# Channel 128's rows by one 89-column matmul a batch, read back once behind the last transform; E and O columns in two tiles

## The chip, the cores and the metric

The kernel runs on one core of a Trainium2 chip. The metric is the device time of one execution in microseconds (us), the median of several runs. The profile is one execution on that core. Its engines are PE (matmuls), PEld (loads of the weight block that a matmul holds still, beside PE), DVE (vector), ACT (scalar), POOL, and SP, which here only issues transfers. "Start-to-start" below is the time from the start of one matmul to the start of the next, read from the start times in the trace. Every run was a fast one, with a mean granted matmul clock of 0.992 or more.

## The reference

```python
def _attn_ref(x):                       # x: 8 x 3008 x 256
    X = np.fft.fft(x, axis=1)
    X = np.fft.fft(X, axis=2)
    return X.real.astype(np.float32)

def _moe_ref(x, w_gate, w_val, w_out):  # x: 24064 x 256, hidden size 1536
    g = x @ w_gate
    gelu = 0.5 * g * (1.0 + erf(g * inv_sqrt2))
    val = x @ w_val
    return (gelu * val @ w_out).astype(np.float32)
```

A two-dimensional Fourier transform per batch, its real part, and a gated feed-forward block on every token.

## The kernel before

The kernel keeps half of the transformed sequence, as even (E) and odd (O) channel parts. From one pair of products it gets a token and its mirror image. Channel 128 belongs to the even side, but it is stored in row 0 of O. Its row is also spread over all 128 partitions (EB), and DVE uses it with one weight per partition (yw) to mend the mirrored value.

The work of the feed-forward block is cut into 288 blocks, 36 a batch (three groups of columns by twelve slices of the hidden size). A block is five matmuls of 512 or 481 columns (L660) and eight of 256 (L749). The transform of the next batch is strewn between them: in each block, behind its matmuls, stand the "fill" steps planned for it. POOL first "folds" the input (sums and differences); `s1t` is the first half of the transform; its result goes through memory and comes back as Z; `tp_e` and `tp_o` make the second half from Z, one each for each of three groups. Where a batch's number stands below beside a stretch of blocks, it is the batch whose transform stands there: batch 4 is blocks 108 to 144. For batches 1 to 7 channel 128 went like this:

```python
    def tp_y(b, gi):                    # once for each of three groups
        ...
            nc.tensor.matmul(
                ps[:4, 0:128], _sub(st["Z"], [[C, 4]], 4 * gi * C + 128), _sub(TP, [[1, 128]], 0),
                start=True, stop=True)
            yr = yrow_tile()
            nc.scalar.activation(yr[:, :], ps[:4, 0:128], AF.Copy)
            y = yrow_dram[b % 2]
            nc.sync.dma_start(
                out=ap_replace(y, ap=[[128, 4], [1, 128]], offset=y.offset + chunk_off[gi]), in_=yr[:, :])

    def tp_rows(b, gi):                 # a block behind the group's tp_o
        ...
            nc.sync.dma_start(out=_sub(EB_bufs[b], [[1, n]], chunk_off[gi]), in_=ap_replace(y, ap=[[0, 128], [1, n]], offset=o))
            nc.sync.dma_start(out=_sub(EO_bufs[b], [[1, n]], HALF + chunk_off[gi], part_num=1), in_=...)
```

The weight block of that matmul is four columns of Z: channel 128 of each of a group's four pairs of sequence positions, 256 elements apart. So a batch has three such matmuls, three evictions by ACT, three row writes to memory and six reads.

## Time and profile before

| | before |
|---|---|
| median of the runs | 630.14 us (629.61 to 630.75) |
| span in the profile | 627.0 us |
| PE, DVE, POOL, ACT busy | 98%, 92%, 81%, 68% |
| a block without fill (512, 481 columns) | 1.95 us, 1.90 us |
| 36 blocks, with the transform of batch 4, 5 or 6 | 73.9 us |
| row matmuls | 21, by shape 128*4 x 128 columns |

The first three lines show a kernel that is bound by its matmul stream. The block times are differences of the starts of each block's first gelu in the trace.

### The profile page before, as it was taken

What the parts mean: (1) busy time and instruction counts of PE and PEld (TensorE: products, weight loads), DVE (VectorE), ACT (ScalarE), POOL (GpSimd) and SP (SyncE); (2) the same over time, 40 slices, a digit from 0 to 9 for tenths busy, and PEclk for the clock granted to TensorE, in tenths of its full rate; (3) what the DMA queues carried; (4) which work ended last, traced back from release to release, by engine and by line L of the source; (5) the groups of instructions that cost most, each with busy time, mean ns of one, the idle gap of its engine ahead of it and who ended that gap; (6) DMA issues with size and microseconds to landing.
All of it is one profiled execution on the core that took longest, in us unless ns stands there. A gap on an engine that the chain in (4) does not pass through costs nothing.

```text
span 627.0 us, 12895 instructions
## 1 busy us (share of the span) xinstructions
PE 612.3 (98%) x4195; PEld 405.1 (65%) x4243; DVE 578.3 (92%) x941; ACT 428.4 (68%) x842; POOL 505.3 (81%) x510
## 2 busy tenths in 40 slices
PE   7999999999999999999999999999999999999997
PEld 3456666666666666666666666666666666666666
DVE  8689989999899999999999998999999999999992
ACT  6777677666776677667676677676676666666661
POOL 8399999989897998879997899969988655555651
PEclk8999999999999999999999999999999999999999
DMA  9961754536353353731645335633212322221123
GB/s 177 227 97 31 210 129 116 144 105 159 99 146 101 98 133 79 184 113 46 160 110 135 101 78 127 148 97 98 62 49 63 91 86 55 51 52 39 42 51 81
DMA packets 54217, 65.40 MB, mean 104 GB/s; under 512 B 7831, under 2 KB 49802, under 8 KB 51754
## 3 DMA queue, kind: packets, MB, share of 16 engines
q1 hardware_dynamic: 47222, 49.03, 30.6%
q0 software_dynamic: 6608, 15.29, 11.4%
q8 instruction: 33, 0.54, 0.4%
q10 hardware_dynamic: 320, 0.26, 0.2%
q14 instruction: 34, 0.28, 0.2%
HBM read 39.65 MB, written 30.17 MB: 111 GB/s over the span
## 4 chain that ended last, share of the span: by engine, by line
PE 93%; ACT 2%; issue 1%; DVE 1%; DMA 1%; POOL 1%; POOLq 0%; ACTq 0%
PE ps_o L749 38%; PE ps_g L660 28%; PE ps_v L660 19%; PE ps_dft L546 2%; PE ps_dft L582 2%; PE ps_o L820 1%; DMA Z_sb<-z 1%; PE ps_dft L443 1%; PE ps_dft L612 0%; ACT gelu_sb L676 0%; POOL h_sb L724 0%; POOL eo_sb L224 0%; DMA out_dram<-out_sb 0%; ACT gelu_sb L685 0%; PE ps_dft L749 0%
## 5 line engine op out<-in xcount | busy, mean ns | idle before, releaser
L724 POOL TENSOR_TENSOR h_sb<-gelu_sb,v_sb 128x512 bf16<-128x512 bf16 (+1 forms) x280 | 319.8, 1146 | 93.1 <-DVE v_sb L722 85.9
L749 PE MATMUL ps_o<-Wo_sb,h_sb 128*128 128x256 bf16 (+1 forms) x2232 | 334.9, 273 | 0.9 <-POOL h_sb L724 0.9
L749 PEld LDWEIGHTS <-h_sb 128*128 128x128 bf16 (+1 forms) x2304 | 228.7, 100 | 112.9 <-POOL h_sb L724 2.6
L676 ACT ACTIVATE gelu_sb<-ps_g 128x512 bf16<-128x512 f32 (+1 forms) x288 | 169.4, 588 | 98.6 <-PE ps_g L660 80.9
L660 PE MATMUL ps_g<-EO_sb,W_sb 128*128 128x512 bf16 (+1 forms) x817 | 228.5, 375 | 3.8 <-ACT gelu_sb L685 0.8
L704 DVE SCALAR_TENSOR_TENSOR ve_sb<-EB_sb,yw,ps_v 128x512 f32<-128x512 bf16 (+1 forms) x280 | 206.3, 737 | 25.9 <-PE ps_v L660 25.0
L660 PE MATMUL ps_v<-EO_sb,W_sb 128*128 128x512 bf16 (+1 forms) x575 | 213.7, 375 | 0.7 <-DVE W_sb L451 0.6
L720 DVE TENSOR_TENSOR h_sb<-gelu_sb,ps_v 128x512 bf16<-128x512 bf16 (+1 forms) x280 | 189.9, 678 | 1.1 <-ACT gelu_sb L685 0.7
L660 PEld LDWEIGHTS <-W_sb 128*128 128x128 bf16 x1440 | 137.2, 98 | 81.1 <-issue 1.8
L722 DVE SCALAR_TENSOR_TENSOR v_sb<-ve_sb,ps_v 128x512 f32<-128x512 f32 (+1 forms) x280 | 187.5, 670 | 0.0
L685 ACT ACTIVATE gelu_sb<-ps_g 128x512 bf16<-128x512 f32 (+1 forms) x288 | 168.7, 586 | 0.0
L769 ACT ACTIVATE out_sb<-ps_o 128x512 f32<-128x512 f32 x92 | 55.0, 598 | 35.7 <-PE ps_o L749 35.6
L224 POOL TENSOR_TENSOR eo_sb<-ab_sb 94x512 bf16<-94x512 f32 (+1 forms) x70 | 77.6, 1111 | 0.5
L549 ACT ACTIVATE S_sb<-ps_dft 96x512 bf16<-96x512 f32 x56 | 32.9, 588 | 14.0 <-PE ps_dft L546 13.9
L592 ACT ACTIVATE EO_sb<-ps_dft 128x512 bf16<-128x512 f32 (+1 forms) x44 | 26.0, 590 | 23.3 <-PE ps_dft L582 22.1
L217 POOL TENSOR_TENSOR ab_sb<-x_raw,x_raw 94x508 f32<-94x508 f32 (+1 forms) x30 | 33.0, 1100 | 0.0
L220 POOL TENSOR_TENSOR ab_sb<-x_raw,x_raw 94x508 f32<-94x508 f32 (+1 forms) x30 | 32.9, 1098 | 0.0
L546 PE MATMUL ps_dft<-eo_sb,G 94*96 94x256 bf16 x119 | 22.5, 274 | 0.2 <-POOL eo_sb L224 0.2
L158 POOL DMA_INDIRECT x_raw<-in_x_dram,idx x18 | 17.1, 948 | 2.9 <-issue 1.1
L582 PE MATMUL ps_dft<-TP,Z_sb 128*128 128x128 bf16 (+1 forms) x184 | 17.8, 218 | 0.0
L582 PEld LDWEIGHTS <-Z_sb 128*128 128x128 bf16 x192 | 14.6, 98 | 1.8 <-DVE Z_sb L534 0.6
L546 PEld LDWEIGHTS <-G 94*96 94x96 bf16 x119 | 13.0, 123 | 1.2 <-issue 0.4
(148 smaller groups left out, 166.2 us busy)
## 6 DMA issues: line engine op xcount, KB each, us to landing
out_dram<-out_sb SPq DMA_DIRECT2D x364, 64.0 KB
x_raw<-in_x_dram SPq DMA_DIRECT2D x10, 768.0 KB
Z_sb<-z SPq DMA_DIRECT2D x7, 768.0 KB
z<-S_sb SPq DMA_DIRECT2D x7, 576.0 KB
EB_sb<-yrow SPq DMA_DIRECT2D x14, 128.0 KB
z<-S_sb SPq DMA_DIRECT2D x7, 192.0 KB
x_raw<-in_x_dram SPq DMA_DIRECT2D x2, 640.0 KB
EB_sb<-yrow SPq DMA_DIRECT2D x7, 120.2 KB
```

The lines of the kernel that those rows point to most:

```text
L224: eng.tensor_tensor(_sub(eo, [[C, nj], [1, 128]], j0 * C + g * 128), ab(0, 0, [[1, 128]]), ab(1, 0, [[1, 128]]), op=op)
L546: nc.tensor.matmul(ps[:96, q * C : (q + 1) * C], G[:, j, :], _sub(eo, [[1, C]], j * C), start=(j == js[0]), stop=(j == js[-1]))
L582: nc.tensor.matmul(ps[:, o : o + n], st["Z"][:, pair, g * 128 : g * 128 + 128], _sub(TP, [[1, n]], g * 128), start=True, stop=True)
L660: nc.tensor.matmul(ps[:, :n], W[nm, part][:, fs], src, start=start, stop=stop, **kw)
L676: nc.scalar.activation(gl[:, 0, :n], pg[:, :n], AF.Gelu)
L685: nc.scalar.activation(_sub(gl, [[-1, n]], TOK + n - 1), pg[:, :n], AF.Gelu)
L704: nc.vector.scalar_tensor_tensor(ve[:, :n], EB_bufs[b][:, c0 : c0 + n], yw[:, fc : fc + 1], pv[:, :n], op0=ALU.mult, op1=ALU.add)
L720: nc.vector.tensor_tensor(st["h"][:, fc, 0, :n], gl[:, 0, :n], pv[:, :n], op=ALU.mult)
L722: nc.vector.scalar_tensor_tensor(_sub(vv, [[-1, n]], n - 1), ve[:, :n], 2.0, pv[:, :n], op0=ALU.mult, op1=ALU.subtract)
L724: nc.gpsimd.tensor_tensor(st["h"][:, fc, 1, :n], gl[:, 1, :n], vv[:, :n], op=ALU.mult)
L749: nc.tensor.matmul(pso[:m, half], st["h"][:, fc, sign, h0 : h0 + m], Wo_sb[:, fc, :], start=(fc == 0 and not (first and sign)), stop=(fc = ...
L769: nc.scalar.activation(_sub(osb, [[1, 2 * C]], 0, part_num=m), pso[:m, :], AF.Copy)
```

## The change

The intent: fewer, wider matmuls for channel 128, fewer transfers, and no wait between transforms and the row's read. There are four parts, of which the fourth is a rearrangement of the plan.

```diff
-    def EO_tile():
-        return work([128, 2, HALF], BF16, "EO", 2, "EO_sb")
+    def EO_tiles():
+        return [work([128, HALF], BF16, t, 2, t + "_sb") for t in ("E", "O")]
...
+    YS = C // 32
+    YM = YS * (NK // 2 - 1) + 1
...
+    def tp_row(b):
+            ps = psum("dft")
             nc.tensor.matmul(
-                ps[:4, 0:128], _sub(st["Z"], [[C, 4]], 4 * gi * C + 128), _sub(TP, [[1, 128]], 0),
+                ps[:YM, 0:128], _sub(st["Z"], [[C // YS, YM]], 128), _sub(TP, [[1, 128]], 0), start=True, stop=True)
             yr = yrow_tile()
-            nc.scalar.activation(yr[:, :], ps[:4, 0:128], AF.Copy)
+            nc.scalar.activation(yr[:, :], ps[:YM, 0:128], AF.Copy)
...
-    def tp_rows(b, gi):
+    def tp_rows(b, c0, n):
...
-    def make_yw(f0, n):                 # four groups, in blocks 0, 1, 2 and 5
+    def make_yw():                      # all twelve, in block 6
...
-            items = []
-            for gi in range(NG):
-                items += [tp_y(b, gi), tp_e(b, gi), tp_o(b, gi)]
+            items = [tp_row(b)] + [f(b, gi) for gi in range(NG) for f in (tp_e, tp_o)]
...
+            if b > 1:
+                at(fill, s + 1, tp_rows(b, 0, HALF))
...
-            first, n = {2: (s0 - 13, 29), 3: (s0 - 19, 30)}.get(b, (s0 - 22, 32))
+            first, n = {2: (s0 - 10, 27), 3: (s0 - 19, 30)}.get(b, (s0 - 22, 32))
...
                 for g in range(2):
                     s = max(s + 1, ready)
+                    while s in taken:
+                        s += 1
                     at(fill, s, s1t(b, jg, g))
```

The wanted rows are 12, one for each pair. The matmul takes 89 columns of Z, 32 elements apart, so every eighth row of its result is wanted and 77 are thrown away. For batch 1 the rows are still read in three pieces. In the opening, two evictions move from DVE to ACT and some output pieces move by a block.

More of the change, by code (lines that the diff above doesn't have):

```diff
@@ L123, in EB_tile @@
         return work([128, HALF], BF16, "EB", 2, "EB_sb")
+    YS = C // 32
+    YM = YS * (NK // 2 - 1) + 1
     def yrow_tile():
-        return work([4, 128], BF16, "yrow", 2, "yrow_sb")
+        return work([YM, 128], BF16, "yrow", 2, "yrow_sb")
     def gelu_tile():
@@ L247 @@
     NGP = NJ * NK
-    ff = work([128, 2 * NGP], FP32, "EO", 2, "ff")
-    rr = work([128, 2 * NGP], FP32, "EO", 2, "rr")
+    ff = work([128, 2 * NGP], FP32, "E", 2, "ff")
+    rr = work([128, 2 * NGP], FP32, "O", 2, "rr")
     rd = work([128, 2 * NGP + NK], FP32, "Z", 1, "rd")
@@ L466, in make_w @@
         return run
-    def make_yw(f0, n):
+    def make_yw():
         def run():
-            c0, nq = f0 // 128, n // 128
             ps = psum("dft")
-            for i in range(nq):
+            for i in range(NFC):
                 nc.tensor.matmul(
-                    ps[:, i : i + 1], W["v", "O"][0:1, f0 + i * 128 : f0 + (i + 1) * 128], one_h,
-                    start=True, stop=True)
-            nc.scalar.activation(yw[:, c0 : c0 + nq], ps[:, 0:nq], AF.Copy)
+                    ps[:, i : i + 1], W["v", "O"][0:1, i * 128 : (i + 1) * 128], one_h, start=True, stop=True)
+            nc.scalar.activation(yw[:, :], ps[:, 0:NFC], AF.Copy)
         return run
@@ L578, in run @@
             if b not in EO_bufs:
-                EO_bufs[b] = EO_tile()
+                EO_bufs[b] = EO_tiles()
             ps = psum(tag) if tag else ps_any(b)
@@ L589, in run @@
             n = chunk_len[gi]
-            dst = _sub(EO_bufs[b], [[1, n]], g * HALF + chunk_off[gi])
+            dst = _sub(EO_bufs[b][g], [[1, n]], chunk_off[gi])
             if engine == "A":
@@ L602, in run @@
             n = chunk_len[gi]
-            eb = _sub(EB_bufs[b], [[1, n]], chunk_off[gi])
             ps = ps_any(b)
-            if b == 0:
-                for pair, o, w in pairs(gi):
-                    nc.tensor.matmul(
-                        ps[:, o : o + w], _sub(st["Z"], [[0, 128]], pair * C + 128), _sub(TP, [[1, w]], 0),
-                        start=True, stop=True)
-                nc.scalar.activation(eb, ps[:, :n], AF.Copy)
-                return
+            for pair, o, w in pairs(gi):
+                nc.tensor.matmul(
+                    ps[:, o : o + w], _sub(st["Z"], [[0, 128]], pair * C + 128), _sub(TP, [[1, w]], 0),
+                    start=True, stop=True)
@@ L612, in run @@
+            nc.scalar.activation(_sub(EB_bufs[b], [[1, n]], chunk_off[gi]), ps[:, :n], AF.Copy)
+        return run
+    def tp_row(b):
+        def run():
+            st = state(b)
+            EB_bufs[b] = EB_tile()
+            ps = psum("dft")
             nc.tensor.matmul(
-                ps[:4, 0:128], _sub(st["Z"], [[C, 4]], 4 * gi * C + 128), _sub(TP, [[1, 128]], 0),
-                start=True, stop=True)
+                ps[:YM, 0:128], _sub(st["Z"], [[C // YS, YM]], 128), _sub(TP, [[1, 128]], 0), start=True, stop=True)
@@ L615, in run @@
             yr = yrow_tile()
-            nc.scalar.activation(yr[:, :], ps[:4, 0:128], AF.Copy)
+            nc.scalar.activation(yr[:, :], ps[:YM, 0:128], AF.Copy)
             y = yrow_dram[b % 2]
+            step = yr.ap[0][0]
             nc.sync.dma_start(
-                out=ap_replace(y, ap=[[128, 4], [1, 128]], offset=y.offset + chunk_off[gi]), in_=yr[:, :])
+                out=ap_replace(y, ap=[[128, NK // 2], [1, 128]], offset=y.offset),
+                in_=ap_replace(yr, ap=[[YS * step, NK // 2], [1, 128]]))
@@ L620, in tp_y @@
         return run
-    def tp_rows(b, gi):
+    def tp_rows(b, c0, n):
         def run():
-            n, y = chunk_len[gi], yrow_dram[b % 2]
-            o = y.offset + chunk_off[gi]
-            nc.sync.dma_start(
-                out=_sub(EB_bufs[b], [[1, n]], chunk_off[gi]), in_=ap_replace(y, ap=[[0, 128], [1, n]], offset=o))
-            nc.sync.dma_start(
-                out=_sub(EO_bufs[b], [[1, n]], HALF + chunk_off[gi], part_num=1),
-                in_=ap_replace(y, ap=[[0, 1], [1, n]], offset=o))
+            y = yrow_dram[b % 2]
+            for dst, rows in ((EB_bufs[b], 128), (EO_bufs[b][1], 1)):
+                nc.sync.dma_start(
+                    out=_sub(dst, [[1, n]], c0, part_num=rows),
+                    in_=ap_replace(y, ap=[[0, rows], [1, n]], offset=y.offset + c0))
@@ L663, in cols_of @@
             n, c0 = chunk_len[ci], chunk_off[ci]
-            E, O = (EO_bufs[b][:, i, c0 : c0 + n] for i in range(2))
+            E, O = (EO_bufs[b][i][:, c0 : c0 + n] for i in range(2))
             if ci not in cstate:
@@ L872, in behind_first_gate @@
     def behind_first_gate():
-        make_yw(0, 256)()
         tp_y(0, 0)()
@@ L886, in plan @@
         for gi in (1, 2):
-            early += [ch(0, 2 * gi), ch(0, 2 * gi + 1, "V"), tp_e(0, gi), tp_o(0, gi, "V"), tp_y(0, gi)]
+            e = "A" if gi == 1 else "V"
+            early += [ch(0, 2 * gi), ch(0, 2 * gi + 1, e), tp_e(0, gi), tp_o(0, gi, e), tp_y(0, gi)]
         for s, f in (
-                (0, make_w(0, 256, 256)), (0, make_w(1, 256, 256, engine="V")), (1, make_yw(256, 256)),
-                (1, make_w(1, 512, 512, (1,))), (2, make_w(0, 512, 512, (0,), "V")), (2, make_yw(512, 512)),
+                (0, make_w(0, 256, 256)), (0, make_w(1, 256, 256, engine="V")),
+                (1, make_w(1, 512, 512, (1,))), (2, make_w(0, 512, 512, (0,), "V")),
                 (3, make_w(0, 512, 512, (1,))), (3, make_w(1, 512, 512, (0,), "V")),
-                (4, make_w(1, 1024, 512, (1,), "V")), (5, make_w(0, 1024, 512, (0,), "V")), (5, make_yw(1024, 512)),
-                (6, make_w(0, 1024, 512, (1,))), (7, make_w(1, 1024, 512, (0,), "V"))):
+                (4, make_w(1, 1024, 512, (1,), "V")), (5, make_w(0, 1024, 512, (0,), "V")),
+                (6, make_w(0, 1024, 512, (1,))), (6, make_yw()), (7, make_w(1, 1024, 512, (0,), "V"))):
             at(fill, s, f)
@@ L901, in plan, with spread @@
             at(fill, s, lambda k=k: load_part(2, k, (load_mirror,)))
-        def spread(b, items, s0, s1):
-            each = len(items) // NG
+        taken = set()
+        def spread(b, s0, s1):
+            items = [tp_row(b)] + [f(b, gi) for gi in range(NG) for f in (tp_e, tp_o)]
             for i, f in enumerate(items):
-                s = s0 + i * (s1 - s0) // (len(items) - 1)
+                s = s0 + (i * (s1 - s0) // (len(items) - 1) if b > 1 else (0, 2, 3, 6, 8, 11, 13)[i])
                 at(fill, s, f)
-                if i % each == each - 1:
-                    at(fill, s + 1, tp_rows(b, i // each))
+                taken.add(s)
+                if b == 1 and i and i % 2 == 0:
+                    at(fill, s + 1, tp_rows(b, chunk_off[i // 2 - 1], chunk_len[i // 2 - 1]))
+            if b > 1:
+                at(fill, s + 1, tp_rows(b, 0, HALF))
         for b in range(1, B):
@@ L937, in plan @@
             at(fill, s + 2, z_read(b))
-            items = []
-            for gi in range(NG):
-                items += [tp_y(b, gi), tp_e(b, gi), tp_o(b, gi)]
             if b == 1:
-                spread(b, items, s + 6, s + 18)
+                spread(b, s + 7, s + 20)
                 continue
             assert s + 7 < s0 + NS - 10
-            spread(b, items, s + 7, s0 + NS - 3)
+            spread(b, s + 7, s0 + NS - 5 if b == 2 else s0 + NS - 6)
         return fill, pool
@@ L957, in feed @@
         first = works[0]
-        sooner = {8: [first[0]], 9: [first[3]], 10: [first[1]], 11: [first[4]], 13: [first[2]], 14: [first[5]]}
+        sooner = {9: [first[0]], 10: [first[3]], 11: [first[1]], 12: [first[4]], 13: [first[2]], 14: [first[5]]}
         works[0] = first[6:]
```

## The prediction

> **What bounds the kernel now.** I read the page first, by engine, then the chain of waits that ended last, then the timeline of a quiet stretch at 290 us, then the list of waits.
>
> ```profile
> PE 612.3 (98%) x4195; PEld 405.1 (65%) x4243; DVE 578.3 (92%) x941; ACT 428.4 (68%) x842; POOL 505.3 (81%) x510
> ...
> PE 93%; ACT 2%; issue 1%; DVE 1%; DMA 1%; POOL 1%; POOLq 0%; ACTq 0%
> PE ps_o L749 38%; PE ps_g L660 28%; PE ps_v L660 19%; PE ps_dft L546 2%; PE ps_dft L582 2%; PE ps_o L820 1%; DMA Z_sb<-z 1%; PE ps_dft L443 1%; PE ps_dft L612 0%; ACT gelu_sb L676 0%; POOL h_sb L724 0%; POOL eo_sb L224 0%; DMA out_dram<-out_sb 0%; ACT gelu_sb L685 0%; PE ps_dft L749 0%
> ```
>
> The matmul engine is busy 98% of 627.0 us and makes 93% of the chain. So the time is the length of the matmul stream: what leaves that stream leaves the time, and what leaves ACT, DVE or the DMA queue counts only where the stream was waiting for it. The row matmuls of channel 128 (L612) look like nothing, 0% of the chain. Their true cost is in the start times of their neighbours:
>
> ```profile
> 291.23 0.60 PE L749 MATMUL ps_o<-Wo_sb,h_sb 128*128 128x256 bf16 x4
> ...
> 291.67 0.39 PE L582 MATMUL ps_dft<-TP,Z_sb 128*128 128x128 bf16 x4
> ...
> 291.89 0.81 PE L660 MATMUL ps_g<-EO_sb,W_sb 128*128 128x512 bf16 x3
> ...
> 293.41 0.60 PE L749 MATMUL ps_o<-Wo_sb,h_sb 128*128 128x256 bf16 x4
> ...
> 293.85 0.81 PE L660 MATMUL ps_g<-EO_sb,W_sb 128*128 128x512 bf16 x3
> ...
> 295.37 0.60 PE L749 MATMUL ps_o<-Wo_sb,h_sb 128*128 128x256 bf16 x4
> ...
> 295.90 0.09 PEld L612 LDWEIGHTS <-Z_sb 128*4 128x4 bf16 x1 [0.21 <-issue]
> 295.90 0.22 PE L612 MATMUL ps_dft<-TP,Z_sb 128*4 128x128 bf16 x1
> ...
> 296.05 0.52 PEld L660 LDWEIGHTS <-W_sb 128*128 128x128 bf16 x4
> 296.05 0.80 PE L660 MATMUL ps_g<-EO_sb,W_sb 128*128 128x481 bf16 x3
> ```
>
> Columns are start and duration in us. Four L749 matmuls with nothing behind them take 293.85 - 293.41 = 0.44 us up to the next L660. With four full transforms (L582) between, 0.66: the four cost 0.22, or 56 ns each. With one row matmul of 4 weight columns between, 0.68: that one costs 0.24. Its weight load stands at 295.90 beside its own matmul, with 0.21 us of idle weight loading before it, where the L749 and L582 loads were done ahead. Over all 21 row matmuls the median start-to-start is 203 ns from the last L749 to L612 (L749 to L582: 109) and 154 ns from L612 to L660 (L582 to L660: 56). So each adds 203 + 154 - 109 = 248 ns, some 190 ns of it for being narrow.
>
> The by-shape groups show that 96 columns are not narrow in this sense, and the list of waits adds up the idle loads and shows one false wait:
>
> ```profile
> L546 PE MATMUL ps_dft<-eo_sb,G 94*96 94x256 bf16 x119 | 22.5, 274 | 0.2 <-POOL eo_sb L224 0.2
> ...
> PEld L612 <- issue: 4.2, 20, 0.2
> ...
> ACT EO_sb L592 <- DMA EO_sb<-yrow: 1.1, 2, 0.6
> ```
>
> L546 (96 weight columns) follows L749 at 109 ns and is followed by L660 at 108 ns, just its own 256 streamed columns: no extra. Idle before the 4-column loads is 0.2 us in 20 cases of 21. In the third line ACT waits to write E or O columns for a row still being read into row 0 of the shared tile.
>
> **What the Trainium skill says.** "TensorE: Matmul & The Clock Gate", section "Back-to-back issue gap", gives N/2.4 + 2.5 ns warm. The trace agrees: 56 ns at 128 columns, 109 at 256, 216 at 512. "TensorEngine Tiling (Array Packing)", section "Key Properties", says: "Mode switching requires drain"; its "Available Configurations" have column tiles of 32, 64 and 128. Four columns would take the 32-column form, 89 the full one. The trace agrees with a drain on the way in (203 for 109) and out (154 for 56), for the 1-column weights of L587 too (136 in, 151 out), and none for 96. The first page's section "Weight-path perf modes" reserves the fast weight load for 128 weights; the trace has 98 ns for 128 columns and 123 ns for the 96 of L546, so 89 columns should load in about 0.12 us (estimate). A stride of 32 elements between weight columns is in no load here.
>
> **The change part by part.**
>
> 1. *Row matmuls.* 3 per batch become 1, for 7 batches; the instruction order of the changed program shows 14 matmuls and 14 weight loads fewer. Removed: 21 x 248 ns = 5.2 us. Added: 7 matmuls of 128 streamed columns, 56 ns each, if no drain comes with 89 columns. Since the matmul is shorter than a weight load, I add some 25 ns for the load of its successor: 7 x 80 ns = 0.6 us. All on the bounding engine: **-4.6 us**.
> 2. *make_yw.* Four groups of 1-row matmuls become one of 12. Entering such a group costs 312 ns where a 512-column matmul alone gives 216 (+96); leaving it takes 91 where the inner ones take 26 (+65). Three groups fewer: 3 x 0.16 = **-0.5 us**, at 19 to 33 us, where the stream waits little.
> 3. *ACT evictions.* 14 of 0.25 us (row) and 3 of yw go; two DVE copies of 0.68 us move to ACT. ACT is busy 68%; only single waits count. **About 0**.
> 4. *E and O in two tiles.* At 160.76 ACT had waited 0.61 us for the row of O before writing E; ACT's two gelus slid, and the stream stood from 162.08 to 162.81, where 0.11 would do. The row now comes after the last transform and E has its own tile: **-0.6 us**, once.
> 5. *Batch 1's slots.* Its first transform step comes one block later. At 80.04 the stream waited 0.26 us for Z's read; that goes. The folds of batch 2 start three blocks later (26 for 23): at 76.94 an L749 waited 1.06 us for POOL, behind those folds. I count half: together **-0.8 us**.
> 6. *DMA.* 14 row writes and 24 row reads fewer; the transfers lie beside compute: **0**, unless the late read is late (below).
> 7. *Opening.* yw leaves ACT, `sooner` and the evictions are shuffled; one ACT wait of 0.33 us at 25.5 may go, others may appear: **0.4 us longer** together with any new wait at a batch's start, as a guard.
>
> Sum: -4.6 - 0.5 - 0.6 - 0.8 + 0.4 = -6.1 us. From 630.1: **624.0 us**, 1.0% less.
>
> **The rivals.**
>
> *The late read becomes a wait.* Rows of batch 2 are read in block 68 and needed in block 72; those of batches 3 to 7 in blocks 103, 139 and so on, needed five blocks later. A block is 1.95 us or more, so there are at least 6 us, then 8. Now, a third of the row (128 KB) has its last packet started 1.3 to 2.7 us after issue, and Z's 768 KB landed 4.2 us after issue, so 376 KB should need 3 us (estimate). Issue usually comes within 1 us of the block's end, but was 3.4 and 4.9 us late in blocks 95 and 100, once behind a row write caught by an input load (5.1 us). That would just touch the deadline in batch 3. If the read is late by 2 us in each of six batches, 12 us come back: about 630. I give this 8%.
>
> *89 strided columns load slowly or drain.* If each new row matmul still costs 250 ns, 1.2 us come back; if a strided load takes 0.4 us, 2 us. Then about 625.5. Against it: L546.
>
> *DVE becomes the bound.* It is busy 92%. Its three operations of a block sum to 2.09 us (737 + 678 + 670 ns), over the 1.95 of a block without extras, yet they overlap by some 0.09 us each: starts at 289.55, 290.15, 290.78. In the last batch, where no transform stands between, the stream still runs at 1.95 us a block, against this rival. It would matter only if blocks fell below 1.9. The gain comes from blocks of 2.2 us and over, so it holds: 5% for losing 2 us.
>
> *Much more comes back.* For a gain over 2% the time must fall below 617.5. All waits of the stream outside the opening that I can name are under 4 us, and part 1 is limited to 5.2. Very unlikely.
>
> **Range and chances.** Part 1 lies between -4.0 and -5.0, the waits between +1 and -3. So 621.8 to 627.0 holds eight times in ten; the spread of the runs before (629.6 to 630.8) adds little. Within 2%: 96%; faster by over 2%: 3%; slower: 1%.
>
> **What the new profile would show.** Part 1: seven row matmuls with 128*89 weights, 109 ns behind L749 and 55 to 110 ns before L660, no idle "issue" line for their loads. Part 2: one yw group. Part 4: no wait of ACT for the row of O, and no 0.7 us stop near 162. Part 5: no stop at 77 and 80. From batch 4 on, a batch, now 73.9 us from start to start, should take 73.3: less 3 x 0.248, plus 0.08. I would be wrong if the O matmul that opens a batch waits for the row's read, if the new row matmul keeps a gap of 0.2 us, or if the opening gets longer by a microsecond or more.

## The result, and the profile after

| | before | after |
|---|---|---|
| median of four runs each | 630.14 us | 623.78 us (622.64 to 624.27) |
| span in the profile | 627.0 us | 620.6 us |

The ratio of the times is 0.9896, 95% interval 0.9879 to 0.9913. Ratios here are the mean time of one kernel's fast runs over that of the other's fast runs of the same rounds, so not quite the ratio of the medians. The gain of 1.0% is clear of the noise.

The page of the kernel after begins so:

```profile
PE 611.3 (98%) x4229; PEld 406.8 (66%) x4229; DVE 576.7 (93%) x939; ACT 425.8 (69%) x827; POOL 504.6 (81%) x510
```

PE's busy time fell by 1.0 us where the span fell by 6.4. The two can't be compared closely: the trace before lacks 48 matmul records that this one has, ends of matmuls are modelled, and much of what went was time between matmuls. The timeline of the matmul engine around one new row matmul (start, us, line; L757 and L668 are the old L749 and L660) shows it:

```profile
280.24 0.38 PE L668 MATMUL ps_v<-O_sb,W_sb 128*128 128x512 bf16 x1
280.46 0.60 PE L757 MATMUL ps_o<-Wo_sb,h_sb 128*128 128x256 bf16 x4
280.89 0.26 PE L621 MATMUL ps_dft<-TP,Z_sb 128*89 128x128 bf16 x1
280.99 0.38 PE L668 MATMUL ps_g<-E_sb,W_sb 128*128 128x512 bf16 x1
```

From the first of four L757 to the next L668 is now 0.53 us, 0.44 without the row matmul, where the old one made it 0.68. In the weight loads of the same stretch, L621's stands before its matmul, with no idle time ahead of it:

```profile
280.24 0.53 PEld L757 LDWEIGHTS <-h_sb 128*128 128x128 bf16 x4
280.79 0.23 PEld L621 LDWEIGHTS <-Z_sb 128*89 128x89 bf16 x1
280.89 0.20 PEld L668 LDWEIGHTS <-W_sb 128*128 128x128 bf16 x2
```

It takes 0.23 us, twice what I had estimated. Over all seven, start-to-start is 109 ns ahead of the row matmul and 97 behind it, 97 ns in all for its presence, against 248 before.

Where the 6.4 us went shows best by stretches of blocks (us, from the starts of the blocks' first gelus; each column is one profiled run):

| blocks | before | after | what stands there |
|---|---|---|---|
| to block 0 | 20.08 | 20.95 | opening, clock still rising; 19.0 to 22.0 in other runs |
| 0 to 12 | 25.46 | 24.38 | weights, yw |
| 12 to 24 | 26.59 | 25.97 | input loads; 25.97 to 27.86 in other runs |
| 24 to 36 | 26.06 | 23.59 | batch 1's transform, batch 2's folds |
| 36 to 48 | 25.37 | 25.75 | |
| 48 to 60 | 23.89 | 24.43 | |
| 60 to 72 | 26.43 | 25.06 | batch 2's transform |
| 72 to 108 | 73.78 | 73.14 | |
| 108 to 144 | 73.92 | 73.43 | |
| 144 to 180 | 73.92 | 73.69 | |
| 180 to 216 | 73.93 | 73.19 | |
| 216 to 252 | 72.91 | 72.59 | |
| 252 to the end | 84.63 | 84.42 | no transform |

Blocks 24 to 72, where batches 1 and 2 are transformed, gave 2.9 us; the five batches behind them gave 2.4 us, where 5 x 0.65 = 3.2 would follow from the row matmuls alone. So there are two things to explain: whether the row matmuls lost time because they were many or because they were narrow, and what held back the last 0.8 us.

### The profile page after: what moved, and what is told of

Same layout as the page of the kernel before. It is cut to its first block, busy times and chain, and to the rows that moved or that the text cites. A ratio compares the mean times of both kernels' runs of the same rounds, so it can differ in the third digit from the quotient of the medians.

```text
span 620.6 us, 12788 instructions
## 1 busy us (share of the span) xinstructions
PE 611.3 (98%) x4229; PEld 406.8 (66%) x4229; DVE 576.7 (93%) x939; ACT 425.8 (69%) x827; POOL 504.6 (81%) x510
## 4 chain that ended last, share of the span: by engine, by line
PE 93%; DVE 2%; DMA 2%; ACT 1%; SPq 1%; issue 1%; POOL 0%; DVEq 0%; ACTq 0%; POOLq 0%
PE ps_o L757 38%; PE ps_g L668 29%; PE ps_v L668 19%; PE ps_dft L549 2%; PE ps_dft L585 2%; PE ps_o L828 1%; SPq L662 1%; DMA out_dram<-out_sb 1%; DMA EB_sb<-yrow 1%; PE ps_dft L448 0%; PE ps_v L395 0%; ACT A_sb L514 0%; PE ps_dft L530 0%; DVE h_sb L724 0%; ACT gelu_sb L684 0%
## 5 line engine op out<-in xcount | busy, mean ns | idle before, releaser
L757 PE MATMUL ps_o<-Wo_sb,h_sb 128*128 128x256 bf16 (+1 forms) x2232 | 334.6, 273 | 0.6 <-POOL h_sb L732 0.6
L757 PEld LDWEIGHTS <-h_sb 128*128 128x128 bf16 (+1 forms) x2304 | 228.7, 100 | 111.7 <-POOL h_sb L732 1.9
L668 PEld LDWEIGHTS <-W_sb 128*128 128x128 bf16 x1440 | 138.0, 98 | 80.8 <-issue 3.2
L668 PE MATMUL ps_g<-O_sb,W_sb 128*128 128x512 bf16 (+1 forms) x576 | 169.1, 375 | 0.1
L693 ACT ACTIVATE gelu_sb<-ps_g 128x512 bf16<-128x512 f32 (+1 forms) x288 | 169.2, 587 | 0.0
L668 PE MATMUL ps_g<-E_sb,W_sb 128*128 128x512 bf16 (+1 forms) x288 | 108.1, 375 | 0.7 <-ACT gelu_sb L693 0.5
L668 PE MATMUL ps_v<-E_sb,W_sb 128*128 128x512 bf16 (+1 forms) x288 | 108.1, 375 | 0.6 <-DVE W_sb L456 0.5
L668 PE MATMUL ps_v<-O_sb,W_sb 128*128 128x512 bf16 (+1 forms) x288 | 108.1, 375 | 0.0
L777 ACT ACTIVATE out_sb<-ps_o 128x512 f32<-128x512 f32 x92 | 55.0, 597 | 35.0 <-PE ps_o L757 34.7
L595 ACT ACTIVATE E_sb<-ps_dft 128x512 bf16<-128x512 f32 (+1 forms) x23 | 13.5, 588 | 8.7 <-PE ps_dft L585 8.7
L595 ACT ACTIVATE O_sb<-ps_dft 128x512 bf16<-128x512 f32 (+1 forms) x22 | 12.9, 588 | 7.3 <-PE ps_dft L585 6.7
```

Of the source, the lines that this page charges most:

```text
L668: nc.tensor.matmul(ps[:, :n], W[nm, part][:, fs], src, start=start, stop=stop, **kw)
L693: nc.scalar.activation(_sub(gl, [[-1, n]], TOK + n - 1), pg[:, :n], AF.Gelu)
L757: nc.tensor.matmul(pso[:m, half], st["h"][:, fc, sign, h0 : h0 + m], Wo_sb[:, fc, :], start=(fc == 0 and not (first and sign)), stop=(fc = ...
L777: nc.scalar.activation(_sub(osb, [[1, 2 * C]], 0, part_num=m), pso[:m, :], AF.Copy)
```

## The experiments

All kernels gave the correct result. Where not said otherwise, a median is of four runs, the kernel before had 7 runs in the same rounds, and all runs named are fast ones (one of the four runs of e3_cols45 was long, 629.16).

### Is it the number of the row matmuls, or their width?

The theory (**drain**): a narrow weight block costs a switch of the matmul array on the way in and out, so width is what matters. The rival (**number**): the gain comes from fewer matmuls, evictions and transfers.

**e1_wide97**: the kernel before, 21 row matmuls as it was, each widened.

```diff
-                ps[:4, 0:128], _sub(st["Z"], [[C, 4]], 4 * gi * C + 128), ...
+                ps[:97, 0:128], _sub(st["Z"], [[C // 32, 97]], 4 * gi * C + 128), ...
-            nc.scalar.activation(yr[:, :], ps[:4, 0:128], AF.Copy)
+            nc.scalar.activation(yr[:, :], ps[:97, 0:128], AF.Copy)
```

(The row write takes every 32nd partition.)

> The kernel before, with each of its 21 row matmuls widened from 4 to 97 weight columns (the wanted rows at every 32nd partition); count, evictions, row writes and reads unchanged. Theory drain (a narrow weight block costs its own switch in and out): a row matmul then adds about 97 ns as the seven of the changed kernel do, or some 105 ns with a longer weight load, in place of 248; 21 x 0.145 = 3.0 us less, 627.1 us. Rival number (the gain came from there being fewer matmuls, evictions and transfers): no change, 630.1 us.

Measured: 627.37 us, ratio 0.996 (0.9934 to 0.9985). Start-to-start became 109 and 121 ns, which makes 21 x 0.127 = 2.7 us. So 21 matmuls that load 97 columns in place of 4, and throw 93 of them away, are 2.9 us cheaper than 21 that load only what is wanted. The number of matmuls, evictions and transfers stayed.

**e2_narrow12** and **e3_cols45**: the changed kernel, one row matmul a batch, with 12 or 45 columns.

```diff
-    YS = C // 32
+    YS = 1          # e2: 12 columns; e3: YS = 4, 45 columns
```

> The changed kernel, with its one row matmul a batch narrowed from 89 to the 12 weight columns that are wanted. Theory drain: 203 ns before it and 154 behind it in place of 109 and 97, so 7 x 0.15 = 1.06 us more than the changed kernel, about 624.8 us. Rival number: no change, or slightly less, since 12 columns load sooner than 89.

Measured: 624.84 us, ratio 0.9917 (0.9897 to 0.9937): 1.06 us over the changed kernel's 623.78, as expected to the second place, though the spread of the runs allows 0.5 either way. Batches 3 to 7 each took 0.17 us more in the trace.

> The changed kernel, with 45 weight columns in its row matmul. Where does narrow begin? If 33 to 64 columns count as narrow like 4 and 12: 203 and 154 ns, 1.06 us more than the changed kernel. If only up to 32 columns do: 109 ns before it, and behind it less than the 97 ns of 89 columns since the load is shorter, so 0 to 0.3 us less.

Measured: 625.31 us, ratio 0.9943 (0.9906 to 0.9981). 45 columns are narrow too, and cost more than 12 by the start times below (the medians, 0.5 us apart, are within the spread of the runs). The views of the row matmul's line in the three kernels (counts, then least, median and greatest duration in ns), first e2, then e3, then the changed kernel:

```profile
L621 PEld LDWEIGHTS <-Z_sb x7: 97/98/98, 81.7 to 503.5; 128*12 128x12 bf16 x7
```
```profile
L621 PEld LDWEIGHTS <-Z_sb x7: 153/153/155, 81.3 to 503.3; 128*45 128x45 bf16 x7
```
```profile
L621 PEld LDWEIGHTS <-Z_sb x7: 229/230/231, 80.0 to 501.0; 128*89 128x89 bf16 x7
```

| kernel | weight columns, elements apart | load, ns | start-to-start ahead, ns | behind, ns | cost, ns |
|---|---|---|---|---|---|
| before | 4, 256 | 85 | 203 | 154 | 248 |
| e2_narrow12 | 12, 256 | 98 | 203 | 168 | 262 |
| e3_cols45 | 45, 64 | 153 | 202 | 224 | 317 |
| after | 89, 32 | 230 | 109 | 97 | 97 |
| e1_wide97 | 97, 8 | 253 | 109 | 121 | 121 |

(Cost is both gaps less the 109 ns that stand there without a row matmul.) Up to 45 columns the load isn't done ahead: some 94 ns pass before it, and the load itself then shows behind. From 89 columns on it is done ahead. Within each kind a longer load costs more. So a weight block below the step costs more than one above it, though its load is shorter.

In this table the narrow blocks also have their columns furthest apart, so distance is a rival. The kernel before answers it in batch 0, where row matmuls (L587) have a single weight column, with no distance. Four of them stand in a row:

```profile
42.46 0.39 PE L582 MATMUL ps_dft<-TP,Z_sb 128*128 128x128 bf16 x4
42.78 0.38 PE L587 MATMUL ps_dft<-TP,Z_sb 128*1 128x128 bf16 x4
43.09 0.61 PE L660 MATMUL ps_g<-EO_sb,W_sb 128*128 128x512 bf16 x2
```

From the last L582 to the first L587 it takes 150 ns where 56 would do (94 more), inside the four 55, and 151 behind. So narrowness alone pays, and it pays on the way in and out and not for each matmul: it is a price of the switch. The step lies between 45 and 89 columns; where, no run shows. What distance does is make the load longer. In e1_wide97 both kinds have 97 columns, adjacent in the first line and 8 elements apart in the second (mean ns behind the bar):

```profile
L750 PEld LDWEIGHTS <-h_sb 128*97 128x97 bf16 x192 | 22.3, 125 | 7.5 <-POOL h_sb L725 0.6 <-DVE h_sb L721 0.2
L612 PEld LDWEIGHTS <-Z_sb 128*97 128x97 bf16 x21 | 5.3, 253 | 0.8 <-DMA Z_sb<-z 0.6
```

### Do the two tiles and the single read matter?

**e4_split_only**: the kernel before with E and O in two tiles, nothing else.

```diff
-            dst = _sub(EO_bufs[b], [[1, n]], g * HALF + chunk_off[gi])
+            dst = _sub(EO_bufs[b][g], [[1, n]], chunk_off[gi])
```

> The kernel before with E and O columns in two tiles and nothing else. Theory: the false wait of ACT for the row's read goes, 0.6 us once near 162 us, so 629.5 us, and ACT waits for EO_sb<-yrow only where it writes O. Rival: ACT still waits, since the evictions of O of the next group come right behind that of E and the row's read goes into O's tile: 630.1 us.

Measured: 628.7 us, ratio 0.9982 (0.9963 to 1.0001), unclear by itself. The trace settles it: blocks 60 to 72 took 25.79 us in place of 26.43, that is 0.64 less; from block 72 to block 252 no stretch differs by more than 0.1; and no ACT wait for a row's read is left in its list. The trace accounts for 0.9 us in all; the rest of the 1.6 us between the medians no trace shows. The wait isn't the same in every kernel with the shared tile: in e8_folds and in e1_wide97 ACT waited 1.4 us for a row's read at 229 to 231 us, and the stream stood 0.8 us behind it, where the kernel before has no such stop.

**e11_groups**: the changed kernel, rows of batches 2 to 7 read in three pieces again.

```diff
-                if b == 1 and i and i % 2 == 0:
+                if i and i % 2 == 0:
...
-            if b > 1:
-                at(fill, s + 1, tp_rows(b, 0, HALF))
```

> The changed kernel, with the rows of batches 2 to 7 read back in three pieces, one behind each group's transforms as before, in place of once a batch. Theory: the transfers are hidden either way, and the gain lies in the matmuls; at most ACT waits again before writing the next group's O columns behind a row's read (0.6 us once or twice): 623.8 to 625. Rival: the single read is what pays; then 12 reads' worth of waits come back and batches 3 to 7 take 73.9 us as before: 626 us or more.

Measured: 623.93 us, ratio 0.9909 (0.9892 to 0.9925), the changed kernel's time. From block 60 to 252 every stretch agrees with it to 0.01 us. Reading once instead of three times buys nothing: those transfers were hidden already.

**e7_late**: the single read three blocks later.

```diff
-                at(fill, s + 1, tp_rows(b, 0, HALF))
+                at(fill, s + 4, tp_rows(b, 0, HALF))
```

> The changed kernel with the late read of batches 2 to 7 issued three blocks later still, one block ahead of its use (none in batch 2). If the read's 3 us are hidden because of the blocks left between, most of them now show: 0 to 1 us at the start of batches 3 to 7 and 2 to 3 us in batch 2, with DVE or the O matmuls waiting for the row: 626 to 629 us. Rival: the row is not needed as soon as its batch starts (buffers of products ahead of DVE), and the time stays at 623.8.

Measured: 632.87 us, ratio 1.0041 (1.0023 to 1.0059), 0.4% slower than the kernel before. I had the sign right and the size wrong: 9 us over the changed kernel, not 2 to 5. The list of what the matmul engine waited for names it:

```profile
PE ps_g L668 <- DMA O_sb<-yrow: 6.8, 2, 6.4
```

(6.8 us in two waits, the longest 6.4, at batch 2; the other, of 0.5, at batch 7.) Blocks 60 to 72 took 31.53 us, 6.5 more than in the changed kernel. The next block lost another 1.9 us, and that is the clock: behind the wait the granted clock was 0.5 from 173.9 to 180.7 us, as the matmul engine's share of two stretches shows (length, PE busy, clock, DMA):

```profile
174.50:180.70 6.20, 3.82 (x15) 0.50 0.67 189
181.00:187.20 6.20, 6.15 (x42) 1.00 0.15 26
```

The matmuls ran at half speed from 176.9 to 180.7 us, 3.8 us, which makes the 1.9. Batches 3 to 7 lost 0 to 0.6.

Why batch 2? In the changed kernel the read's last packet ends 3.3 to 3.6 us after issue. It is issued 8.5 to 9.4 us ahead of the first matmul that reads O from batch 3 on, but only 3.2 us ahead in batch 2: nothing is left there. The reason is the queue of SP, in time order (changed kernel):

```profile
163.66 2.38 SPq L662 DMA_DIRECT2D out_dram<-out_sb  x4
166.15 0.53 SPq L636 DMA_DIRECT2D EB_sb<-yrow  x1
166.72 0.30 SPq L636 DMA_DIRECT2D O_sb<-yrow  x1
```

Block 68, in which batch 2 reads, is one that finishes an output tile, and its four writes are issued first. In e7 the read moves to block 71, another such block. There it was issued 6.1 us later than in the changed kernel, counted from the start of block 60 in each, and so 2.9 us after the matmul should have started; that matmul started 3.7 us after the issue, and 2.9 + 3.7 is, but for rounding, the 6.5 us. I had expected 2 to 3 us because I took the landing alone, as if the issue were on time, and had no thought of the clock.

### The opening: yw in one group

**e6_yw4**: the changed kernel with yw in four groups, in blocks 0, 1, 2 and 5.

```diff
-                (6, make_w(0, 1024, 512, (1,))), (6, make_yw()), ...
+                (1, make_yw(256, 256)), (2, make_yw(512, 512)), (5, make_yw(1024, 512)), ...   # and (0, 256) behind the first gate
```

> The changed kernel with yw made again in four groups in blocks 0, 1, 2 and 5, as before. The first twelve blocks took 25.46 us before and 24.38 after. Theory: the groups' switching (3 x 0.16 us) and the one ACT wait behind them (0.3 to 0.4 us) make most of that 1.08: the first twelve blocks take 25.2 to 25.4 and the time is 0.5 to 1.0 us over the changed kernel, 624.5 us. Rival: the opening gained by chance of the start, and this kernel keeps 24.4.

Measured: 624.09 us, ratio 0.9896 (0.9877 to 0.9914), no difference by the runs. In the trace blocks 0 to 12 took 25.03 us, so yw accounts for 0.65 of the 1.08 us gained there; the other 0.4 are the opening's other moves, which I didn't take apart. Other runs of the unaltered opening gave 24.38, 24.39 and 24.54, and 24.94 in e11_groups, so one profile of it is good to about half a microsecond and this reading is weak.

### Two waits in a row

**e8_folds**: the kernel before with only batch 2's folds three blocks later.

```diff
-            first, n = {2: (s0 - 13, 29), 3: (s0 - 19, 30)}.get(b, (s0 - 22, 32))
+            first, n = {2: (s0 - 10, 27), 3: (s0 - 19, 30)}.get(b, (s0 - 22, 32))
```

> The kernel before, with only the folds of batch 2 three blocks later (from block 26 to 51 in place of 23 to 50). Theory: of the 2.5 us that blocks 24 to 36 lost between the two kernels, 1.06 are the stop for POOL at 77 us, and these go with the folds: blocks 24 to 36 take 25.0 in place of 26.06 us, and the time is 629.2 us if nothing comes back behind. Rival: POOL's work only stands elsewhere, and a stop of the same kind shows near 100 us as in the changed kernel: 630.1 us in all.

Measured: 629.32 us, ratio 0.9996 (0.9976 to 1.0015), the same. Neither side was quite right. The stop for POOL at 77 us went, but no stop for POOL came near 100 us. The one behind it, for Z's read, grew instead. The timelines of the matmul engine, of before and then of e8 (in brackets: idle before, and what ended it):

```profile
78.11 0.28 PE L749 MATMUL ps_o<-Wo_sb,h_sb 128*128 128x256 bf16 x1 [0.89 <-POOL h_sb L724]
...
80.51 0.22 PE L612 MATMUL ps_dft<-TP,Z_sb 128*4 128x128 bf16 x1 [0.19 <-DMA Z_sb<-z]
```
```profile
79.21 0.60 PE L749 MATMUL ps_o<-Wo_sb,h_sb 128*128 128x256 bf16 x4
81.00 0.22 PE L612 MATMUL ps_dft<-TP,Z_sb 128*4 128x128 bf16 x1 [1.19 <-DMA Z_sb<-z]
```

Before, 1.06 us of waiting for POOL hid most of the wait for Z. Take the first away and 1.26 us of the second show at once (start-to-start less the usual). The changed kernel moves the folds and starts the transform a block later. Together they pay; the folds alone do not, and the later start alone was not run.

### What held back the last 0.8 us

The trace of the changed kernel has 16 places, from batch 3's to batch 7's transform, where the first matmul of a block starts 0.13 to 0.15 us late; the kernel before has 7 such places in its whole run. One of the 16, in the timeline of all engines:

```profile
358.51 0.60 ACT L777 ACTIVATE out_sb<-ps_o 128x512 f32<-128x512 f32 x1 [0.38 <-PE ps_o L757]
...
359.00 0.59 ACT L595 ACTIVATE E_sb<-ps_dft 128x512 bf16<-128x512 f32 x1
...
359.48 0.60 ACT L684 ACTIVATE gelu_sb<-ps_g 128x512 bf16<-128x512 f32 x1
...
359.95 0.62 ACT L693 ACTIVATE gelu_sb<-ps_g 128x512 bf16<-128x512 f32 x1
360.04 0.60 PE L757 MATMUL ps_o<-Wo_sb,h_sb 128*128 128x256 bf16 x4
...
360.62 0.38 PE L668 MATMUL ps_g<-E_sb,W_sb 128*128 128x512 bf16 x1
```

ACT has four evictions in one block: a finished output tile (L777, every third block), a transform (L595) and two gelus. The gate matmul at 360.62 needs the buffer that L693 frees, which ended at 360.57; 109 ns behind the last L757 would have been 360.48. (The profile names no releaser for this stop; that it is ACT is read from these times, and e9 tests it.) Of the 60 blocks of batches 3 to 7 that evict an output tile, 10 also have an E or O eviction in the new plan; in the old one it was 2, and 9 had the short eviction of a row.

**e9_slots**: the changed kernel, with those steps of batches 3 to 7 kept out of blocks whose number leaves 2 on division by 3.

```diff
+                while b > 2 and (s in taken or s % 3 == 2):
+                    s += 1
                 at(fill, s, f)
...
-                    while s in taken:
+                    while s in taken or (b > 2 and s % 3 == 2):
                         s += 1
```

> The changed kernel, but for batches 3 to 7 no transform or folding step stands in a block whose number leaves 2 on division by 3, where ACT also evicts a finished output tile. Theory: the gate matmul that stood 0.14 us, three times a batch, waited for ACT behind four evictions in one block; those stops go and a batch takes 73.1 instead of 73.2 to 73.7: 1 to 2 us less, 622.3 us. Rival: the stops come from elsewhere or only move; no change, 623.8.

Measured: 622.04 us, ratio 0.9874 (0.9853 to 0.9895). Batches 4, 5 and 6 took 72.95 us each, to the hundredth, where the changed kernel has 73.43, 73.69 and 73.19; of the 16 stops one is left. This is 1.7 us under the changed kernel by the medians, 1.6 us by the sum of blocks 72 to 252. The 15 stops that went add up to 2.1 us, so they do not come back one for one.

**e10_both**: e9, and the first piece of batch 1's broadcast rows read two blocks earlier.

```diff
+            if b == 1:
+                at(fill, s0 + 2, tp_rows(b, 0, chunk_len[0], (0,)))
```

> As e9_slots, and the first group of batch 1's broadcast rows is read right behind the write of the row, two blocks earlier, with only its O row where it was. Theory: in the changed kernel DVE waited 0.8 us for that read at 96 us and the stream lost 0.8 us at 100 us; both go, blocks 36 to 48 take 25.0 instead of 25.75: 0.8 us less than e9_slots, 621.5 us. Rival: the stop at 100 us belongs to POOL's folds and stays; no change from e9_slots.

Measured: 621.37 us (620.98 to 622.36), ratio 0.9855 (0.9838 to 0.9872). My reading of the chain falls. DVE's wait of 0.8 us for the row's read at 96 us is gone from the list, yet the stop behind it is there as before: blocks 36 to 48 took 25.73 us. First the changed kernel, then e10:

```profile
101.17 0.28 PE L757 MATMUL ps_o<-Wo_sb,h_sb 128*128 128x256 bf16 x1 [0.64 <-POOL h_sb L732]
```
```profile
102.88 0.28 PE L757 MATMUL ps_o<-Wo_sb,h_sb 128*128 128x256 bf16 x1 [0.61 <-POOL h_sb L732]
```

The stop is for POOL. The folds of batch 2 now stand here, but that they set it is not shown: e8 had them in the same blocks and no such stop. The chain led through DVE's wait, which did not set the time. The 0.7 us by which e10's median lies below e9's are within their spread, and no stretch past block 72 differs between the two. So e9's rule is what beats both kernels, and e10 is at least as good.

## Why the prediction was right

The predicted time was 624.0 us and the measured 623.78, within the range. Step by step:

- **Part 1, the row matmuls** (-4.6): right in mechanism and nearly in size. e1, e2 and e3 show that the width of the weight block sets the price, and the four L587 that it is paid at the switch; that the array drains there is the prediction's reading of it. The start-to-start times give 21 x 0.248 less 7 x 0.097 = 4.53 us. The load was mis-sized (0.12 us estimated, 0.23 measured), so a new row matmul costs 97 ns rather than 80, 0.12 us in all. That rival, a slow strided load, was real but small.
- **Part 2, yw** (-0.5): 0.65 us in one profile of e6, no difference in its times; in keeping, not shown.
- **Part 3, ACT's evictions** ("about 0"): this missed something. Which block an eviction falls in matters where ACT gets four in one block. The stops of 0.14 us total 2.3 us in the changed kernel against 0.9 before, so 1.4 us were given back, and e9 removed them. Part 7's guard of +0.4 was meant for the opening and the starts of batches, not for this.
- **Part 4, two tiles** (-0.6): 0.64 us in e4's trace. Where and how long this wait falls is partly chance: e8 and e1, with the same shared tile, lost 0.8 us to it at another place.
- **Part 5, batch 1's slots** (-0.8): the two stops at 77 and 80 us are gone, 1.3 us together, and one of 0.8 us for POOL stands at 100 us. By these stops 0.5 us is left net; by the stretches it is 1.0 (2.9 us of blocks 24 to 72 less 1.3 for two batches' row matmuls and 0.6 for part 4). The forecast lies between. That the two waits stood in a row, so that moving the folds alone pays little, was not foreseen; e8 showed it.
- **Part 6, transfers** (0): e11 shows it to 0.01 us a stretch. The late read is not a wait in the changed kernel. I had counted some 6 us of lead for batch 2, and it has 3.2, against a landing of 3.4. The estimate of 3 us for the landing was about right, the estimate of the lead was not: the read stands behind four output writes. That it didn't show was close to luck, and e7 shows what a delay there costs.
- **From batch 4 on 73.3 us a batch**: 73.43, 73.69 and 73.19 were measured, for the reason given under part 3.

The sum came out right partly by luck, because terms offset each other: up to block 24 the profile is 0.8 us shorter where parts 2 and 7 come to 0.1, blocks 24 to 72 gained 2.9 where 2.7 were forecast, and blocks 72 to 252 gained 2.4 where 3.3 were. To what extent the first 24 blocks gained by the change can't be told from single profiles, since the same opening scattered by a microsecond or two between runs.

## What to carry to other kernels

Price a small matmul by the start times of its neighbours, not by its own duration: here 21 matmuls at 0% of the chain cost 5.2 us, and loading columns that nobody wants was cheaper than loading few. A wait can cost more than its length: e7's of 6.4 us was followed by 6.8 us at half clock. When moving steps about on an engine that isn't the bound, count what falls into each single block, since four evictions in one block stopped the matmul stream though ACT was busy 69%. And when a wait is removed, look at the next wait behind it on the same path before counting the gain.

## What the Trainium skill lacked or had wrong

- "TensorEngine Tiling (Array Packing)", section "Key Properties", says that a change of tiling mode drains, without a price. If that is what happens here (no run shows the mode), it cost 94 ns on the way in (203 for 109 ns), and on the way out the whole load showed (154 to 224 ns start-to-start, growing with the columns). Nor does the page say that an ordinary matmul with few weight columns is treated so without being asked: 1, 4, 12 and 45 columns paid, 89, 96 and 97 did not, in line with its column tiles of 32, 64 and 128.
- "TensorE: Matmul & The Clock Gate", section "LDWEIGHTS (loading the stationary operand)", gives columns/1.2 ns, whatever the distance between columns. Measured: 97 adjacent columns 125 ns (formula: 81), 97 columns 8 elements apart 253. The others were 85 ns for 4 columns, 98 for 12, 153 for 45 and 230 for 89, at distances of 256, 256, 64 and 32 elements: about 80 ns plus 1.7 ns a column where they are apart. (Only this section is meant; other pages of the skill do treat spaced reads.)
- No page has that a stop for a full buffer can come from which block an eviction is planned into, on an engine with spare time; 15 of 16 stops of 0.14 us went when e9 moved evictions out of such blocks.
